# Attention and low-rank mixer on one core: loads in one queue, the first batch reordered, two up blocks begun early, the q gain moved behind the last V, the last tile in three

## The chip, the cores and the metric

The kernel runs on 1 core of one Trainium2 chip. The metric is the device time of one execution in microseconds (us). An execution is also profiled; its time lies beside its span (from the first to the last recorded instruction). The engines are TensorE (PE, matmuls; PEld is its weight load), VectorE (DVE), ScalarE (ACT), GpSimd (POOL) and SyncE (SP, which here only issues DMAs). Each engine works through its own instructions in the order in which the program gives them.

## The reference

```python
# q, k, v: (8, 12, 448, 64); U: (448, 32); V: (32, 448); w_ch1: (768, 3072); w_ch2: (3072, 768)
q_n, k_n = rmsnorm(q, g_q), rmsnorm(k, g_k)            # x / sqrt(mean(x * x) + 1e-6) * g
attn = softmax(q_n @ k_n.T / sqrt(64))                 # by head
x = (attn @ v).transpose(0, 2, 1, 3).reshape(8, 448, 768)
u = x + (x.transpose(0, 2, 1) @ U @ V).transpose(0, 2, 1)
out = u + relu(u @ w_ch1) @ w_ch2                      # float32
```

## The kernel before

**Attention.** The 12 heads of a batch form three groups of four, 24 groups in all; two heads that are worked on together are a pair (`pr`), six pairs in a batch. Per group: `load` brings q, k and v in float32; `squares`, `sums` (L133) and `roots` (L139, L140) give the scale of each row; `scale` or `scale_dma` multiply q and k by it into bfloat16 (`qn`, `kp`); then q and k are transposed into `qT` and `kz`. Groups 0 to 5 are transposed by PE (`turn`) and copied by `take_q`, with the product g_q g_k folded in, and `take_k`. From group 6 on the DMA transposes them (`turn_dma`), and `take_dma` (L341) multiplies `qT` by g_q g_k in place on VectorE. `Sc(b, pr, r)` computes a row block of scores, transposed, two matmuls of 448 columns (L365), and its exponential E on ACT (L366); a pair has four of them, the fourth of half size. `V(b, pr, half)` multiplies E by v with a column of ones (L378, L382), and VectorE takes the reciprocal of the sums (L385) and writes x (L386).

**Mixer and MLP.** For batch 0, `mix_t0` and `mix` compute u transposed (`uT`) on PE, six blocks of 128 of the 768 columns, with copies on ACT or VectorE; for later batches `mix_t` (pu, cast to tb at L401), `mix_tr` (pw, copied to tT at L408) and `mix_rows` (pm, added at L456) compute u, and the DMA transposes it. `up(b, ht)` is one of 24 blocks of the hidden layer: six matmuls over the blocks of `uT` (L466), relu on ACT (L468). `down` computes 128 rows of the output by 384 columns in 24 matmuls (L479), cut into four parts that other work may stand between; VectorE adds u (L487), and two DMAs of 64 rows each on SP's queue write the result (L495), after both halves.

**Order.** The order of the instructions is written out. The first batch's attention is a hand-made list, `extra`, keyed by (pair, row block). After it two lists exist: `att`, the attention of the batches to come, and `mlp`, the mixer and MLP. Each entry has a cost in us, which only serves the planner at the end: it emits the next `att` entry if the costs emitted so far are not ahead of `due`, otherwise the next `mlp` entry. An entry of cost 0 thus follows its predecessor only when the next entry is due: it comes out right in front of that. In the middle of `att`:

```python
        if a == 1 and more and by_dma:
            add_att(0.0, take_dma, gi + 1)
        add_att(0.19, Sc, b, pr, 3)
        if a == 0 and not by_dma:
            add_att(0.0, scale_all, gi + 1)
        if pr != 0:
            add_att(0.55, V, *pairs[i - 1], 1)
```

**Start.** q of group 0 is loaded on SP's queue, k on ACT's, and g_q and g_k behind it on ACT's, then the table of the activation functions. PE runs 115 matmuls on an identity matrix (`keep_busy`, L208) ahead of its first work. VectorE clears the empty parts of `kz` and `vl`, POOL those of Vm (L276), Uz (L290) and tb (L297) while the first data come in.

Of the kernel before, what the change touches and what calls it, by code (L numbers as in the profile page):

```python
# [9 lines left out]
FP32 = mybir.dt.float32  # L10
# [3 lines left out]
ALU = AluOpType  # L14
# [10 lines left out]
def kernel(  # L25
# [13 lines left out]
    nc = tc.nc  # L39
# [14 lines left out]
    D1 = D + 1  # L54
    KD = dm // P
    KH = dh // P
    NPAIR = H // 2
    HALF = dm // 2
    scal = 1.0 / (D ** 0.5)
# [126 lines left out]
    for gi in range(3):  # L186
        stage_tiles(gi)
    load_qk(0, 0)
    load_qk(0, 1, nc.scalar)
    for i, g in enumerate((g_q, g_k)):  # L190
        nc.scalar.dma_start(grow[:, i, :], g.rearrange("(o d) -> o d", o=1))
    for i in range(2):
        load_qk(1, i)
    load_qk(2, 0)
# [16 lines left out]

    eps = consts.tile([P, 1], FP32)
    nc.vector.memset(eps, 1e-6)
    for va, vl in zip(va_bufs, vl_bufs):
# [4 lines left out]
    for t in kz_bufs:  # L219
        for a in range(2):  # L220
            nc.vector.memset(t[D:P, a, :S], 0.0)
            nc.vector.memset(t[0:D, a, S:], 0.0)

    gg = consts.tile([P, 2], FP32)
    bias = gg[:, 1:2]
# [47 lines left out]
    for m in range(NQ):  # L273
        nc.sync.dma_start(Vf[m * rank:(m + 1) * rank, :], moe_V)

    nc.gpsimd.memset(Vm, 0.0)  # L276

    def prep_v(lo, hi):
        for m in range(lo, hi):
# [10 lines left out]
    nc.gpsimd.memset(Uz, 0.0)  # L290
# [5 lines left out]
    for t in tb_bufs:  # L296
        nc.gpsimd.memset(t, 0.0)  # L297


    qk, es, xs = {}, {}, {}  # L300
# [132 lines left out]

    u_rest = consts.tile([P, dm], BF16)

    def urows(b, col, half):
        h = slice(half * HALF, (half + 1) * HALF)
        return u_rest[:, h] if col == SM else xs[b][:, (col - (0 if b % 2 else R)) // P, h]

    def mix_rows(b, w, half):  # L440

        odd = b % 2
# [19 lines left out]
    def up(b, ht):  # L462
# [4 lines left out]
                             start=(dt == 0), stop=(dt == KD - 1))  # L467
        nc.scalar.activation(hT[:, ht, off:off + S], ph, AF.Relu)  # L468

    down_ps, down_sb = {}, {}  # L470

    def down(b, col, half, part, nparts):
        key = (b, col, half)
        if part == 0:
            down_ps[key] = ps.tile([P, HALF], FP32, name="po", tag="ps")
        po = down_ps[key]
        n = KH // nparts
        for ht in range(part * n, (part + 1) * n):
            nc.tensor.matmul(po, hT[:, ht, col:col + P], w2b[:, ht, half * HALF:(half + 1) * HALF],  # L479
                             start=(ht == 0), stop=(ht == KH - 1))  # L480
        if part < nparts - 1:
            return
        h = slice(half * HALF, (half + 1) * HALF)
        if half == 0 or b == 0:
            down_sb[(b, col)] = outp.tile([P, dm], FP32, name="ob", tag="ob")
        ob = down_sb[(b, col)]
        nc.vector.tensor_tensor(ob[:, h], po, urows(b, col, half), ALU.add)  # L487
        if half == 1 or b == 0:
            h = h if b == 0 else slice(0, dm)

            def rows(b, j):
                return out[b].rearrange("(p j) d -> j p d", j=NT)[j]
            for i in range(2):
                o = rows(b, i * NJ + col // P) if col != SM else rows(b - i, 2 * NJ)
                nc.sync.dma_start(o[:, h], ob[i * R:(i + 1) * R, h])  # L495


    pairs = [(b, pr) for b in range(B) for pr in range(NPAIR)]
# [18 lines left out]
    def scales(gi):  # L517
        return [(0, roots, (gi,)), (0, scale, (gi, 0, pool)), (0, scale, (gi, 1, pool))]

    def turns(gi):  # L520
        return [(0.4, turn, (gi, 0)), (0, take_q, (gi, 0)), (0, take_q, (gi, 1)), (0.4, turn, (gi, 1)), (0, take_k, (gi, 0))]
# [4 lines left out]
        (0, 2): [(0, keep_busy, (8,))],  # L526
        (0, 3): [(0, keep_busy, (8,))],
        (1, 1): [V2(0, 0)],
        (1, 2): [(0, sums, (2, 0))] + turns(1),
        (1, 3): [V2(0, 1), (0, sums, (2, 1)), (0, take_k, (1, 1)), (0, values, (1,)), (0, load, (4,)),  # L530
                 (0, weights, (1,))],
        (2, 1): scales(2) + [(0, weights, (1,)), V2(1, 0)],
        (2, 3): [V2(1, 1)],
        (3, 1): [V2(2, 0)],
        (3, 2): turns(2),
        (3, 3): [V2(2, 1), (0, take_k, (2, 1)), (0, values, (2,)), (0, load, (5,)), (0, prep_v, (0, 1)), (0, prep_u, ()),
                 (0, weights, (1,)), (0, squares, (3, 0, pool)), (0, squares, (3, 1, pool)), (0, weights, (1,))],
        (4, 1): [V2(3, 0)],
        (4, 3): [V2(3, 1), (0, sums, (3, 0))],
        (5, 0): [(0.9, mix_t0, (0, 512))],  # L540
        (5, 1): [V2(4, 0), (0.39, mix, (0, 0))],
        (5, 2): [(0.39, mix, (0, 1)), (0.39, mix, (0, 2))],
        (5, 3): [V2(4, 1), (0.39, mix, (0, 3)), (0, prep_v, (1, NQ)), (0, weights, (2,))],
    }
    for i in range(NPAIR):
        for r in range(4):
            add_att(0.38, Sc, *pairs[i], r)
            att.extend(extra.get((i, r), []))
    att.extend([V2(5, 0), V2(5, 1), (0.45, mix_t0, (512, dm, True)), (0, sums, (3, 1)), (0, roots, (3,)),
                (0.39, mix, (0, 4, True)), (0.39, mix, (0, 5))])  # L550
    first_done = len(att)

    att.extend([(0, scale, (3, 0, pool)), (0, scale, (3, 1, nc.vector)), (0, values, (3,)), (1.0, lambda: None, ()), (0.4, turn, (3, 0)), (0.4, turn, (3, 1)),
                (0, take_q, (3, 0)), (0, take_q, (3, 1)), (0, take_k, (3, 0)), (0, take_k, (3, 1))])

    for i, (b, pr) in enumerate(pairs):
        if b == 0:
            continue
        gi, a = divmod(i, 2)
        more = gi + 1 < len(groups)  # L560
        by_dma = gi + 1 >= DMA_FROM
        soon = gi + 2 < len(groups)

        if pr == 0 and b > 1:
            add_att(0.55, V, *pairs[i - 1], 0)
            add_att(0.55, V, *pairs[i - 1], 1)
        add_att(0.38, Sc, b, pr, 0)
        if i == 2 * DMA_FROM - 2:
            add_att(0.0, load, DMA_FROM + 1)
        if a == 0 and not by_dma:  # L570
            add_att(0.0, squares, gi + 1, 0, nc.gpsimd)
            add_att(0.0, squares, gi + 1, 1, nc.gpsimd)
            if gi + 2 >= DMA_FROM:
                add_att(0.0, load, gi + 2)
        add_att(0.38, Sc, b, pr, 1)
        if pr != 0:
            add_att(0.55, V, *pairs[i - 1], 0)
        if a == 1 and more and not by_dma:
# [12 lines left out]
        if a == 1 and more and not by_dma:  # L591
            add_att(0.39, T, gi + 1, 1)
        if a == 1 and more and by_dma:
            add_att(0.0, take_dma, gi + 1)
        add_att(0.19, Sc, b, pr, 3)
        if a == 0 and not by_dma:
            add_att(0.0, scale_all, gi + 1)
        if pr != 0:
            add_att(0.55, V, *pairs[i - 1], 1)
        if a == 1 and soon and gi + 2 >= DMA_FROM:  # L600
            add_att(0.0, sums, gi + 2, 0)
            add_att(0.0, sums, gi + 2, 1)
            add_att(0.0, scale_all, gi + 2)
# [10 lines left out]
    PRE = (16, 20)  # L614
    mlp = []
    for b in range(B):
        for ht in range(KH):
            mlp.append((1.14, up, (b, ht), b))
            if b < ROWS_FROM and ht % 2 == 0 and ht < 4 * NW:
                mlp.append((0.17, mix_rows, (b, ht // 4, ht // 2 % 2), b))  # L620
        cols = (64, 192, 320) if b % 2 == 0 else (384, 0, 128, 256)
        n = len(cols) * 8
        nb = b + 1
        pre = {}
        if ROWS_FROM <= nb < B:
# [5 lines left out]
        tiles = [(col, half) for col in cols for half in range(2)]  # L631
        if b == 0:
            tiles.sort(key=lambda t: t[1])
        for c, (col, half) in enumerate(tiles):
            for part in range(4):
                mlp.extend(pre.get(c * 4 + part, []))
                mlp.append((0.98, down, (b, col, half, part, 4), b))

    for i in range(2):
        squares(0, i)  # L640
# [9 lines left out]
    nc.vector.tensor_copy(gg, pg)  # L650
    squares(1, 0)
    squares(1, 1)
    values(0)
    squares(2, 0, nc.gpsimd,
            uT.rearrange("p k c -> p (k c)")[:, :4 * NT * D].bitcast(FP32).rearrange("p (j d) -> p j d", d=D))
# [86 lines left out]
```

## Time and profile before

| what | value |
|---|---|
| runs | 607.54, 604.35, 608.5 us; median 607.54 |
| profiled execution | 602.04 us, span 600.3 us |
| granted TensorE clock | 1.0 |
| PE / DVE / ACT / POOL busy | 586.2 / 206.6 / 312.5 / 158.5 us |
| matmuls: down (L479), up (L466), scores (L365), V (L382) | 241.6, 237.1, 93.7, 57.2 us |
| first scores on PE | 12.15 us |
| last matmul ends | 595.53 us |

The page gives busy time by engine, then the span in slices, the queues, the chain of work that ended last, and groups of instructions by source line. A timeline line gives start and duration in us, engine, line, operation, output<-input and shape; in brackets stands how long the engine had been idle and what released it. A line of the windows gives the window, its length, busy time of PE, PEld, DVE, ACT and POOL with the number of instructions, the granted clock, the DMA engines' share and GB/s.

### The profile page before, as it was taken

To read this page: it belongs to the slowest core of one execution; us is meant where nothing else is said; L and a number is where in the kernel's file an instruction comes from. 1 tells how busy PE (TensorE), PEld (TensorE's weight loads), DVE (VectorE), ACT (ScalarE), POOL (GpSimd) and SP (SyncE) were. 2 spreads that over 40 slices of the span, in tenths; PEclk is the share of its full clock that TensorE was granted. 3 is DMA by queue.
4 is the path that set the end of the run, shared out by engine and by line. 5 is a ranking of instruction groups with operands and counts; after the bars stand their busy time and mean duration, and the time that the engine had idled before them with its cause. 6 is when DMAs were issued, how large, how long until landed. Compare 5 with 4: busy or idle time off the path is not lost.

```text
span 600.3 us, 11625 instructions
## 1 busy us (share of the span) xinstructions
PE 586.2 (98%) x4807; PEld 357.9 (60%) x4807; DVE 206.6 (34%) x474; ACT 312.5 (52%) x479; POOL 158.5 (26%) x271
## 2 busy tenths in 40 slices
PE   8889999999999999999999999999999999999996
PEld 8555656655666556655566655665566655655563
DVE  6686535511343322531235321541234310320011
ACT  6857873477453776356744477346763344004300
POOL 7997633123213303303303312302312000000000
PEclk9999999999999999999999999999999999999999
DMA  9999996784295454675256746277305310230022
GB/s 257 221 243 246 242 199 160 149 204 96 53 206 107 132 124 113 112 179 123 48 134 99 189 116 139 58 174 169 50 2 89 84 27 0 54 72 2 0 54 52
DMA packets 118360, 71.70 MB, mean 119 GB/s; under 512 B 80420, under 2 KB 115108, under 8 KB 118308
## 3 DMA queue, kind: packets, MB, share of 16 engines
q1 hardware_dynamic: 108304, 61.04, 45.0%
q0 software_dynamic: 9728, 9.47, 9.5%
q8 instruction: 37, 0.61, 0.4%
q10 hardware_dynamic: 276, 0.46, 0.2%
q14 instruction: 15, 0.12, 0.1%
HBM read 52.20 MB, written 11.01 MB: 105 GB/s over the span
## 4 chain that ended last, share of the span: by engine, by line
PE 92%; DVE 3%; ACT 2%; DMA 1%; POOL 1%; issue 0%; POOLq 0%; DVEq 0%; ACTq 0%
PE po L479 36%; PE ph L466 35%; PE sc L365 9%; PE pv L382 5%; PE pm L451 2%; PE pv L378 1%; PE busy L208 1%; ACT E L366 1%; DMA qT<-qn 1%; DVE ssq L133 1%; PE pu L399 1%; PE pt L311 1%; DVE x L386 0%; DVE kz L326 0%; POOL sq L130 0%
## 5 line engine op out<-in xcount | busy, mean ns | idle before, releaser
L479 PE MATMUL po<-w2b,hT 128*128 128x384 bf16 x1344 | 241.6, 326 | 1.0 <-DVE x L386 1.0
L466 PE MATMUL ph<-uT,w1b 128*128 128x448 bf16 x1152 | 237.1, 352 | 0.0
L366 ACT ACTIVATE E<-sc,gg 128x896 bf16<-128x896 f32 x192 | 171.9, 911 | 75.3 <-PE sc L365 75.1
L479 PEld LDWEIGHTS <-hT 128*128 128x128 bf16 x1344 | 126.9, 98 | 79.2 <-DVE x L386 1.1
L466 PEld LDWEIGHTS <-w1b 128*128 128x128 bf16 x1152 | 109.7, 98 | 96.1
L468 ACT ACTIVATE hT<-ph 128x448 bf16<-128x448 f32 x192 | 104.0, 545 | 116.7 <-PE ph L466 114.6
L162 POOL TENSOR_TENSOR qn<-qf,rs 128x384 bf16<-128x384 f32 x36 | 29.9, 830 | 279.1 <-ACT rs L140 225.4
L365 PE MATMUL sc<-qT,kz 128*128 128x448 bf16 x336 | 93.7, 352 | 5.2 <-ACT E L366 3.5
L385 DVE RECIPROCAL r<-pv 128x4 f32<-128x4 f32 x96 | 17.4, 181 | 212.2 <-PE pv L382 211.7
L382 PE MATMUL pv<-va,E 128*128 128x65 bf16 x1152 | 57.2, 194 | 0.0
L487 DVE TENSOR_TENSOR ob<-po,x 128x384 f32<-128x384 f32 x48 | 26.8, 558 | 84.6 <-PE po L479 83.4
L382 PEld LDWEIGHTS <-E 128*128 128x128 bf16 x1152 | 50.5, 98 | 7.5
L133 DVE TENSOR_REDUCE ssq<-sq 128x14 f32<-128x896 f32 x47 | 48.8, 1076 | 2.2 <-ACT sq L128 1.7
L365 PEld LDWEIGHTS <-kz 128*128 128x128 bf16 x336 | 31.8, 98 | 29.1 <-issue 4.7
L378 PE MATMUL pv<-vl,E 128*128 128x130 bf16 x192 | 42.1, 219 | 0.0
L386 DVE TENSOR_TENSOR x<-pv,r 128x256 bf16<-128x256 f32 x96 | 40.8, 425 | 3.3
L139 ACT ACTIVATE rs<-ssq,eps 128x28 f32<-128x28 f32 (+1 forms) x25 | 7.9, 318 | 52.4 <-DVE ssq L133 41.1
L456 DVE TENSOR_TENSOR x<-pm,x 128x384 bf16<-128x384 f32 x48 | 26.6, 554 | 17.9 <-PE pm L451 16.8
L162 POOL TENSOR_TENSOR kp<-kf,rs 128x384 bf16<-128x384 f32 x36 | 29.9, 829 | 0.0
L378 PEld LDWEIGHTS <-E 128*128 128x128 bf16 x192 | 18.7, 97 | 8.1 <-issue 1.2
L170 POOL CAST va<-vf 128x768 bf16<-128x768 f32 x24 | 20.7, 863 | 2.0 <-DMA vf<-in_v_dram 2.0
L128 ACT ACTIVATE sq<-qf 128x896 f32<-128x896 f32 x20 | 18.8, 942 | 2.3 <-DMA qf<-in_q_dram 2.3
(84 smaller groups left out, 265.2 us busy)
## 6 DMA issues: line engine op xcount, KB each, us to landing
qf<-in_q_dram SPq DMA_DIRECT2D x24, 448.0 KB, 4.2
kf<-in_k_dram SPq DMA_DIRECT2D x23, 448.0 KB, 5.5
out_dram<-ob SPq DMA_DIRECT2D x50, 192.0 KB, 2.7
vf<-in_v_dram SPq DMA_DIRECT2D x48, 192.0 KB, 5.4
w1b<-in_moe_w_ch_dram POOLq DMA_DIRECT2D x4, 1152.0 KB, 17.1
w2b<-in_moe_w_ch_dram POOLq DMA_DIRECT2D x8, 576.0 KB, 17.5
vf<-in_v_dram SPq DMA_DIRECT2D x48, 32.0 KB, 4.9
out_dram<-ob SPq DMA_DIRECT2D x12, 96.0 KB, 2.5
```

What stands on the lines that cost most here:

```text
L133: nc.vector.tensor_reduce(ssqs[gi][:, i, :], sqs.pop((gi, i)), AX, ALU.add)
L162: nc.gpsimd.tensor_tensor(main.rearrange("p (t i) d -> p i t d", i=2), src[:, c, :2 * NJ].rearrange("p (i t) d -> p i t d", i=2), rs[:, c, ...
L365: nc.tensor.matmul(sc[:, i, :S], kz[:, c:c + P], qT, start=True, stop=True)
L366: nc.scalar.activation(es[(b, pr)][:, 2 * r:2 * r + n, :], sc[:, :n, :S], AF.Exp, scale=scal, bias=bias)
L378: nc.tensor.matmul(pv[:, i].rearrange("p e d -> p (e d)"), E[:, NJ, w:w + P], vl[:, lp, :], start=True, stop=False)
L382: nc.tensor.matmul(pv[:, i, e, :], E[:, e * (NJ + 1) + j, w:w + P], va[:, (lp + 2 * e) * NJ + j, :], start=False, stop=(e == 1 and j == NJ ...
L386: nc.vector.tensor_tensor(xs[b].rearrange("p i (h d) -> p i h d", d=D)[:, 2 * half:2 * half + 2, h0:h0 + 3:2, :], pv[:, :, :, :D], r.rearr ...
L456: nc.vector.tensor_tensor(dst, ph[lo:hi], x[lo:hi], ALU.add)
L466: nc.tensor.matmul(ph, w1b[:, dt, ht * P:(ht + 1) * P], uT[:, dt, off:off + S], start=(dt == 0), stop=(dt == KD - 1))
L468: nc.scalar.activation(hT[:, ht, off:off + S], ph, AF.Relu)
L479: nc.tensor.matmul(po, hT[:, ht, col:col + P], w2b[:, ht, half * HALF:(half + 1) * HALF], start=(ht == 0), stop=(ht == KH - 1))
L487: nc.vector.tensor_tensor(ob[:, h], po, urows(b, col, half), ALU.add)
```

## The change

There are five parts.

1. The first loads: k of group 0 and g_q, g_k are issued on SP's queue. `fill_k` clears `kz`: the first buffer on VectorE ahead of the other fills, the second on POOL; POOL's fills of Uz, Vm and tb become `fill_mixer`, emitted after the squares of group 1.
2. The first batch: group 1's turns go ahead of its `sums(2, 0)`, `scales(2)` comes at (2, 0) instead of (2, 1), `sums(3, 0)` and the mix blocks come one place later, the fourth mix block is copied by ACT, and `roots(3)` follows the last mix block.
3. `up_begin` runs four of the six matmuls of up blocks 0 and 1 of batch 0 before the mixer of the last four heads is done, into two banks of a score buffer; `up_end` runs the other two and the relu, after up block 2.
4. `take_dma` follows the pair's second V instead of standing in front of the fourth `Sc`.
5. The last output tile is computed in pieces of 384, 192 and 192 columns, each written alone, with the second row half issued on ACT's queue.

```diff
-    load_qk(0, 1, nc.scalar)
+    load_qk(0, 1)
     for i, g in enumerate((g_q, g_k)):
-        nc.scalar.dma_start(grow[:, i, :], g.rearrange("(o d) -> o d", o=1))
+        nc.sync.dma_start(grow[:, i, :], g.rearrange("(o d) -> o d", o=1))
...
+    fill_k(kz_bufs[0], nc.vector)
...
-    nc.gpsimd.memset(Vm, 0.0)
+    fill_k(kz_bufs[1], nc.gpsimd)
...
+    def fill_mixer():
+        nc.gpsimd.memset(Uz, 0.0)
+        nc.gpsimd.memset(Vm, 0.0)
+        for t in tb_bufs:
+            nc.gpsimd.memset(t, 0.0)
...
+    def up_begin(b, ht):
+        off = 64 if b % 2 == 0 else 0
+        if not begun:
+            begin = ps_sc.tile([P, 2, 512], FP32, name="sc", tag="sc")
+            begun.update({(b, i): begin[:, i, :S] for i in range(2)})
+        for dt in range(KD_EARLY):
+            nc.tensor.matmul(begun[(b, ht)], w1b[:, dt, ht * P:(ht + 1) * P], uT[:, dt, off:off + S],
+                             start=(dt == 0), stop=False)
...
-        if half == 1 or b == 0:
-            h = h if b == 0 else slice(0, dm)
+        if hi == dm or alone:
+            h = slice(lo if alone else 0, hi)
...
-                nc.sync.dma_start(o[:, h], ob[i * R:(i + 1) * R, h])
+                (nc.scalar if alone and i and b else nc.sync).dma_start(o[:, h], ob[i * R:(i + 1) * R, h])
...
-        (1, 2): [(0, sums, (2, 0))] + turns(1),
+        (1, 2): turns(1) + [(0, sums, (2, 0))],
...
-        (2, 1): scales(2) + [(0, weights, (1,)), V2(1, 0)],
+        (2, 0): scales(2) + [(0, weights, (1,))],
+        (2, 1): [V2(1, 0)],
...
-        (4, 3): [V2(3, 1), (0, sums, (3, 0))],
+        (4, 3): [V2(3, 1)],
         (5, 0): [(0.9, mix_t0, (0, 512))],
-        (5, 1): [V2(4, 0), (0.39, mix, (0, 0))],
-        (5, 2): [(0.39, mix, (0, 1)), (0.39, mix, (0, 2))],
-        (5, 3): [V2(4, 1), (0.39, mix, (0, 3)), (0, prep_v, (1, NQ)), (0, weights, (2,))],
+        (5, 1): [V2(4, 0), (0, sums, (3, 0))],
+        (5, 2): [(0.39, mix, (0, 0)), (0.39, mix, (0, 1))],
+        (5, 3): [V2(4, 1), (0.39, mix, (0, 2)), (0.39, mix, (0, 3, True)), (0, prep_v, (1, NQ)), (0, weights, (2,))],
...
-    att.extend([V2(5, 0), V2(5, 1), (0.45, mix_t0, (512, dm, True)), (0, sums, (3, 1)), (0, roots, (3,)),
-                (0.39, mix, (0, 4, True)), (0.39, mix, (0, 5))])
+    att.extend([V2(5, 0), V2(5, 1), (0.76, up_begin, (0, 0)), (0.45, mix_t0, (512, dm, True)),
+                (0, sums, (3, 1)), (0.76, up_begin, (0, 1)), (0.39, mix, (0, 4, True)), (0.39, mix, (0, 5)), (0, roots, (3,))])
...
-        if a == 1 and more and by_dma:
-            add_att(0.0, take_dma, gi + 1)
         add_att(0.19, Sc, b, pr, 3)
         if a == 0 and not by_dma:
             add_att(0.0, scale_all, gi + 1)
         if pr != 0:
             add_att(0.55, V, *pairs[i - 1], 1)
+        if a == 1 and more and by_dma:
+            add_att(0.0, take_dma, gi + 1)
...
-        for ht in range(KH):
-            mlp.append((1.14, up, (b, ht), b))
+        for ht in (2, 0, 1, *range(3, KH)) if b == 0 else range(KH):
+            mlp.append((0.38, up_end, (b, ht), b) if b == 0 and ht < 2 else (1.14, up, (b, ht), b))
...
+    for lo, hi in ((0, HALF), (HALF, HALF + 192), (HALF + 192, dm)):
+        mlp.append((3.9 * (hi - lo) / HALF, down, (B - 1, cols[-1], lo, hi, 0, 1, True), B - 1))
...
+    fill_mixer()
     values(0)
```

More of the change, by code (lines that the diff above doesn't have):

```diff
@@ L56 @@
     KH = dh // P
+    KD_EARLY = 4
     NPAIR = H // 2
@@ L213, with fill_k @@
     nc.vector.memset(eps, 1e-6)
+    def fill_k(t, eng):
+        for a in range(2):
+            eng.memset(t[D:P, a, :S], 0.0)
+            eng.memset(t[0:D, a, S:], 0.0)
+    fill_k(kz_bufs[0], nc.vector)
     for va, vl in zip(va_bufs, vl_bufs):
@@ L218 @@
             nc.vector.memset(vl[e * R:(e + 1) * R, :, e * D1 + D:(e + 1) * D1], 1.0)
[L219 to L222, printed above, removed]
     gg = consts.tile([P, 2], FP32)
@@ L289 @@
     tz = first[:, 1, :]
-    nc.gpsimd.memset(Uz, 0.0)
     def prep_u():
@@ L295 @@
     tb_bufs = [consts.tile([P, 2 * P], BF16, name=f"tb{i}") for i in range(2)]
-    for t in tb_bufs:
-        nc.gpsimd.memset(t, 0.0)
+    def fill_mixer():
[3 more added lines that the diff above has]
+            nc.gpsimd.memset(t, 0.0)
     qk, es, xs = {}, {}, {}
@@ L434 @@
     u_rest = consts.tile([P, dm], BF16)
-    def urows(b, col, half):
-        h = slice(half * HALF, (half + 1) * HALF)
-        return u_rest[:, h] if col == SM else xs[b][:, (col - (0 if b % 2 else R)) // P, h]
     def mix_rows(b, w, half):
@@ L468, in up, with up_end, down @@
         nc.scalar.activation(hT[:, ht, off:off + S], ph, AF.Relu)
+    begun = {}
+    def up_begin(b, ht):
[6 more added lines that the diff above has]
+                             start=(dt == 0), stop=False)
+    def up_end(b, ht):
+        off = 64 if b % 2 == 0 else 0
+        for dt in range(KD_EARLY, KD):
+            nc.tensor.matmul(begun[(b, ht)], w1b[:, dt, ht * P:(ht + 1) * P], uT[:, dt, off:off + S],
+                             start=False, stop=(dt == KD - 1))
+        nc.scalar.activation(hT[:, ht, off:off + S], begun[(b, ht)], AF.Relu)
     down_ps, down_sb = {}, {}
-    def down(b, col, half, part, nparts):
-        key = (b, col, half)
+    def down(b, col, lo, hi, part, nparts, alone):
+        key = (b, col, lo)
         if part == 0:
             down_ps[key] = ps.tile([P, HALF], FP32, name="po", tag="ps")
-        po = down_ps[key]
+        po = down_ps[key][:, :hi - lo]
         n = KH // nparts
         for ht in range(part * n, (part + 1) * n):
-            nc.tensor.matmul(po, hT[:, ht, col:col + P], w2b[:, ht, half * HALF:(half + 1) * HALF],
-                             start=(ht == 0), stop=(ht == KH - 1))
+            nc.tensor.matmul(po, hT[:, ht, col:col + P], w2b[:, ht, lo:hi], start=(ht == 0), stop=(ht == KH - 1))
         if part < nparts - 1:
             return
-        h = slice(half * HALF, (half + 1) * HALF)
-        if half == 0 or b == 0:
+        if lo == 0 or b == 0:
             down_sb[(b, col)] = outp.tile([P, dm], FP32, name="ob", tag="ob")
         ob = down_sb[(b, col)]
-        nc.vector.tensor_tensor(ob[:, h], po, urows(b, col, half), ALU.add)
-        if half == 1 or b == 0:
-            h = h if b == 0 else slice(0, dm)
+        u = u_rest if col == SM else xs[b][:, (col - (0 if b % 2 else R)) // P]
+        nc.vector.tensor_tensor(ob[:, lo:hi], po, u[:, lo:hi], ALU.add)
+        if hi == dm or alone:
+            h = slice(lo if alone else 0, hi)
             def rows(b, j):
@@ L548 @@
             att.extend(extra.get((i, r), []))
-    att.extend([V2(5, 0), V2(5, 1), (0.45, mix_t0, (512, dm, True)), (0, sums, (3, 1)), (0, roots, (3,)),
-                (0.39, mix, (0, 4, True)), (0.39, mix, (0, 5))])
+    att.extend([V2(5, 0), V2(5, 1), (0.76, up_begin, (0, 0)), (0.45, mix_t0, (512, dm, True)),
+                (0, sums, (3, 1)), (0.76, up_begin, (0, 1)), (0.39, mix, (0, 4, True)), (0.39, mix, (0, 5)), (0, roots, (3,))])
     first_done = len(att)
-    att.extend([(0, scale, (3, 0, pool)), (0, scale, (3, 1, nc.vector)), (0, values, (3,)), (1.0, lambda: None, ()), (0.4, turn, (3, 0)), (0.4, turn, (3, 1)),
-                (0, take_q, (3, 0)), (0, take_q, (3, 1)), (0, take_k, (3, 0)), (0, take_k, (3, 1))])
+    att.extend([(0, scale, (3, 0, pool)), (0, scale, (3, 1, nc.vector)), (0, values, (3,)), (0.7, lambda: None, ()), (0.4, turn, (3, 0)), (0.4, turn, (3, 1)),
+                (0, take_q, (3, 0)), (0, take_q, (3, 1)), (0, take_k, (3, 0)), (0, take_k, (3, 1)), (0.3, lambda: None, ())])
     for i, (b, pr) in enumerate(pairs):
@@ L630 @@
                     pre[n - PRE[nb > 1] + 2 + 2 * w + half] = [(0.17, mix_rows, (nb, w, half), nb)]
-        tiles = [(col, half) for col in cols for half in range(2)]
+        tiles = [(col, half * HALF, (half + 1) * HALF, b == 0) for col in cols for half in range(2)]
         if b == 0:
             tiles.sort(key=lambda t: t[1])
-        for c, (col, half) in enumerate(tiles):
+        for c, tile_ in enumerate(tiles):
+            if b == B - 1 and c >= len(tiles) - 2:
+                continue
             for part in range(4):
                 mlp.extend(pre.get(c * 4 + part, []))
-                mlp.append((0.98, down, (b, col, half, part, 4), b))
+                mlp.append((0.98, down, (b, *tile_[:3], part, 4, tile_[3]), b))
+    for lo, hi in ((0, HALF), (HALF, HALF + 192), (HALF + 192, dm)):
+        mlp.append((3.9 * (hi - lo) / HALF, down, (B - 1, cols[-1], lo, hi, 0, 1, True), B - 1))
     for i in range(2):
```

## The prediction, made before the changed kernel had run

> **What bounds the kernel now.** I read the page first: busy time by engine, and the chain that ended last.
>
> ```profile
> PE 586.2 (98%) x4807; PEld 357.9 (60%) x4807; DVE 206.6 (34%) x474; ACT 312.5 (52%) x479; POOL 158.5 (26%) x271
> PE 92%; DVE 3%; ACT 2%; DMA 1%; POOL 1%; issue 0%; POOLq 0%; DVEq 0%; ACTq 0%
> ```
>
> TensorE (PE) is busy for all but 14.1 of 600.3 us. No edit takes matmul work away, so the change is worth the idle time that it closes minus the idle time that it opens. The windows tell where there is idle time to close (PE's busy time is the first figure after the window's length).
>
> ```profile
> 0.00:15.00 15.00, 13.15 (x167) 12.15 (x167) 10.50 (x35) 9.12 (x14) 10.96 (x22) 1.00 0.95 257
> 15.00:30.00 15.00, 12.12 (x160) 8.22 (x158) 10.44 (x33) 13.28 (x20) 13.52 (x15) 1.00 0.97 221
> 30.00:45.00 15.00, 12.85 (x144) 8.31 (x144) 13.11 (x26) 8.36 (x14) 14.10 (x18) 1.00 1.14 242
> 180.00:585.00 405.00, 405.00 (x3148) 242.30 (x3147) 114.56 (x251) 197.66 (x306) 71.48 (x143) 1.00 0.42 91
> 585.00:600.30 15.30, 10.52 (x65) 6.12 (x63) 1.68 (x3) 0.00 (x0) 0.00 (x0) 0.99 0.20 51
> ```
>
> About 7 us are lost before 45 us, 4.8 at the end, and nothing in the 405 us between 180 and 585: whatever stalls PE there is paid in full. The timeline names the gaps that the change aims at (the bracket holds the idle time before the line and its releaser).
>
> ```profile
> 38.95 0.39 PE L414 MATMUL pu<-x 128*128 128x256 bf16 x2 [0.44 <-DVE x L386]
> 40.33 0.36 PE L424 MATMUL ph<-Vm,x 128*128 128x448 bf16 x1 [0.46 <-ACT x L416]
> 80.01 0.54 PE L365 MATMUL sc<-qT,kz 128*128 128x448 bf16 x2 [0.60 <-ACT E L366]
> 91.74 0.45 DVE L341 TENSOR_SCALAR qT<-qT,gg 128x896 bf16<-128x896 bf16 x1 [5.18 <-DMA qT<-qn]
> 92.80 4.07 PE L479 MATMUL po<-w2b,hT 128*128 128x384 bf16 x24 [0.98 <-DVE x L386]
> ```
>
> **The change, part by part.**
>
> *Start: 0.* k's load goes behind q's on SP instead of on ACT's queue, g_q and g_k follow on SP, ACT's table load (1.28 us) is no longer behind three issues, and VectorE clears only one kz buffer before its sums. q, k and their scales may come about a microsecond sooner. But PE runs 115 warm-up matmuls until 10.13, then pg and the q turn at 10.67 and the k turn at 11.11; q's scale ends at 10.11 and k's at 11.06. The first scores follow PE's own order, so sooner data bring nothing. If this cover were gone, the gain would be at most the 0.6 us between the end of k's scale and the kz copy at 11.72. On POOL the fills of Uz, Vm and tb (0.57 + 1.85 + 0.61 = 3.0 us) move behind q's scale, 10.11 at the latest, so they end between 11.6 and 13.1; the cast of v, at 12.07 now, is used only after some rows of scores. I take 0, with -0.6 to +0.5.
>
> *First batch: 0.* The turns of group 1 ahead of sums(2, 0) release the scores at 20.55 about 0.5 sooner (wait on kz: 0.52). Against it, roots(2) now stands on ACT in front of E of the same rows and waits for sums(2, 1), 2 x 1.08 us on VectorE behind the copies: E comes about 1.1 later, of which 0.5 falls into ACT's idle time. sums(3, 0) leaves the place ahead of the tz copy, which frees the 0.62 wait at 34.74. Sum -0.1, rounded to 0; bounds -0.6 to +0.7.
>
> *Two up blocks begun: -1.1, lost again by 80.* Eight matmuls (4 of 6 in each block; six take 1.14 at L466, so 8 x 0.19 = 1.52 us) go into the idle 0.44 + 0.15 + 0.46 at 38.95 to 40.33. That is all they can fill: 1.05. They remove no work. After it roots(3) stands behind the last mix copy, so q's scale on POOL (1.69 from 41.18 now) ends later while its turn comes sooner; of the gain some is waited out there, but the 0.48 wait for kz at 46.11 goes. I get PE 1.1 further by 46. Then comes a chain whose length PE does not set: from the turn of k at 72.38 through the kz copies, the clearing of kp (0.81), V's pair, two sums (2.07), roots(6) and E, to the scores at 80.01, 7.63 us. PE waits 0.60 there now. With PE further on in the up blocks, one block fewer (1.14) lies inside that chain, so the wait grows by that: 0.60 + 1.14 = 1.74. I keep -0.1 of -1.1 (bounds -1.1 and +0.8, where the wait at the turns of group 3 stays).
>
> *g_q g_k behind the last V: -1.0, then +6.1.* take_dma (L341, one VectorE multiply, 0.44 us, x18) moves from ahead of the fourth row of scores to behind the second V. Today at 86.5 it waits 5.18 us for a DMA, and V's pair of L385 and L386 behind it keeps PE waiting 0.98 at 92.80. In the new order V goes first, so this 0.98 is won, once; at no other L341 does VectorE wait for a DMA.
>
> But the multiply now stands directly in front of the scores that need it, behind whatever VectorE has just been given. Reading the new order of PE and VectorE beside each other, group by group, I counted the matmuls between the source of the VectorE operation ahead of the multiply and the new group's first scores. In the old order there were 3.6 us or more of them. In the new one there are none for groups 7, 10, 13 (a down block's add ahead) and 19 (the tb cast ahead). The place for group 7 is visible already:
>
> ```profile
> 112.14 2.11 PE L479 MATMUL po<-w2b,hT 128*128 128x384 bf16 x12
> 114.09 0.54 PE L365 MATMUL sc<-qT,kz 128*128 128x448 bf16 x2
> ```
>
> ```profile
> 111.16 0.44 DVE L341 TENSOR_SCALAR qT<-qT,gg 128x896 bf16<-128x896 bf16 x1
> 114.29 0.56 DVE L487 TENSOR_TENSOR ob<-po,x 128x384 f32<-128x384 f32 x1 [1.31 <-PE po L479]
> 114.76 2.07 DVE L133 TENSOR_REDUCE ssq<-sq 128x14 f32<-128x896 f32 x2
> ```
>
> The scores start at 114.09, since qT was multiplied 3 us before. In the new order the multiply sits between L487 and L133: it starts at 114.76 as L133 does now, takes 0.44, and some 0.05 later (as the kz copy of 11.72, 0.38 long, frees the scores at 12.15) the scores start: 114.76 + 0.44 + 0.06 - 114.09 = 1.17. Groups 10 and 13 have the same rows (add at 180.48 and 247.00, scores at 180.28 and 246.80): 3 x 1.17 = 3.5. Group 19 has the cast (0.36) in the add's place: 1.0. Groups 17, 20 and 22 have one quarter of a down block (0.98) between: 1.17 - 0.98 = 0.2 each, 0.6. Group 23 has an add and a half u_rest add ahead, and 1.15 of matmuls: 0.5. In group 16 the two sums (2.07) now lie between the tb cast and the tT copy, which pm waits for: 0.4. The other groups have 2 us or more of matmuls there: 0. Sum 3.5 + 1.0 + 0.6 + 0.5 + 0.4 = 6.0, less 0 for cover, since PE idles nowhere in that stretch. Bounds: 2.3 (each of the four bare places gets a quarter of a down block, 0.2) and 7.
>
> *The last tile in 384, 192, 192: -1.2.* After PE's last matmul (595.53) there are now:
>
> ```profile
> 595.56 0.56 DVE L487 TENSOR_TENSOR ob<-po,x 128x384 f32<-128x384 f32 x1 [3.34 <-PE po L479]
> ```
>
> then two SP issues that end at 596.61 and 597.25, and landings at 598.76 and 599.34. The last add shrinks to 192 columns: 0.36, as the cast of 192 columns, -0.2. The second issue goes to ACT's queue, beside the first: -0.6. The pieces shrink from 192 KB; the page has 2.7 us from issue to landing for 192 KB and 2.5 for 96 KB, so -0.2 at least, and -1.0 if the last bytes at 300 GB/s bound the end (393 KB in 1.3 us, 98 KB in 0.3). 24 more matmuls of half width add 0.05. Sum -0.95 to -1.75; I take -1.2. The Trainium skill's DMA: Bandwidth & Descriptors (Rules for kernel authors) says that transfers under 64 KB pay mostly overhead; the new pieces have 48 KB, and by it the byte term would be 0 and the sum -0.75. The 0.2 between the two rows here leans its way, but no 48 KB row stands in this trace.
>
> **Sum:** 0 + 0 - 0.1 - 1.0 + 6.0 - 1.2 = +3.7 us on the profiled execution's 602.04 (span 600.3): 605.7. The runs of before have their median at 607.54, 5.5 above that execution; the same +3.7 there gives 611.2.
>
> **Rivals.**
> *Faster or level: the bare places are covered.* If PE has something else at the four places (the order of the down quarters slips by one as PE's lead changes) each costs 0.2: 0.8 + 0.6 + 0.5 + 0.4 = 2.3, all 0.0, 607.5. If the multiply never delays scores, the sum is -2.3: 605.2; if, besides, the early lead is kept at 80 (-1.1 for -0.1) and the end gives 1.75, -3.9: 603.6. For it: scores of groups that start with two V's have cover. Against it: both engines' orders are fixed in the program, and the rows at 114 leave no room. It decides at group 7's first scores.
> *Slower still: the early stage.* roots(2) and roots(3) are later on ACT, and POOL, 13 to 14 us busy in each 15 us there, gets the fills late. If the kept -0.1 becomes +0.8, the first batch +0.7, the start +0.5 and a split end only -0.75, the sum is +3.7 + 2.5 + 0.45: +6.7, 614.2. For it: ACT and POOL at 13.28 and 13.52 of 15. Against it: PE's gaps of before 45 us belong to several waits, and one delay is often paid by another's slack.
> *The begun blocks fill nothing:* PE then reaches 80 later with a shorter wait there, so the end hardly moves: +3.8, 611.3. It shows only in the early gaps.
>
> **Chances.** Forecast (+1 to +6) 0.55; covered, level or faster 0.17; slower still 0.25; the rest 0.03. A measurement of this kernel tells about 1% (6 us) from no change. Over 1% faster needs more than the whole first rival: 0.08. Over 1% slower is the second rival and the upper edge of the forecast: 0.32. Within 1%: 0.60. The range runs from the first rival's lower end, 604, to 617, above the second rival by the 7 for 6 of the multiply and 2 for what I may not have seen.
>
> **What would show it.** Right: PE idle of 1.1 to 1.2 us ahead of the first scores of groups 7, 10 and 13, released by qT's multiply, and about 1.0 at group 19; no 0.98 at 92.8; a larger wait for E near 80; the span 0.8 to 1.8 us shorter behind the last matmul; 180 to 585 no longer full. Wrong: that stretch still full of PE (then the first rival), or over 3 us more idle before 90 (then the second).

## The result, and the profile after

The changed kernel takes 613.0 us (median of 5 runs, 612.04 to 614.22) beside 606.9 us for the kernel before (604.35 to 608.5): ratio 1.0105, interval 1.0074 to 1.0137. A second set of runs gave 610.9 beside 604.58 us: 1.0108 (1.0081 to 1.0134). The prediction was 611.2 in a range of 604 to 617. Its profiled execution took 612.44 us (span 610.7), 10.4 more than the shown one of before, but that one was among the fastest of before, whose later runs lie between 601.4 and 608.2 us. So the sum of the steps is to be judged by the 6 us of the medians, and its terms by the traces.

The page of the changed kernel: more idle time on PE, less PE in the chain that ended last.

```profile
PE 588.2 (96%) x4830; PEld 359.0 (59%) x4831; DVE 205.2 (34%) x470; ACT 313.3 (51%) x480; POOL 160.0 (26%) x275
PE 89%; DVE 3%; DMA 2%; issue 2%; ACT 1%; POOL 1%; SPq 0%; POOLq 0%; DVEq 0%
```

Its windows (PE's busy time first, the granted clock third from the end): 15 to 30 lost 2.5 us more than before, 45 to 60 lost 1.9 more with the clock at 0.89, and the stretch behind 100, which was full, is no longer full (87.89 of 90 us in the last line).

```profile
15.00:30.00 15.00, 9.67 (x126) 6.45 (x126) 8.06 (x22) 10.79 (x15) 13.66 (x12) 1.00 0.95 229
30.00:45.00 15.00, 13.39 (x163) 8.84 (x160) 12.72 (x30) 9.37 (x15) 11.78 (x18) 1.00 1.14 242
45.00:60.00 15.00, 12.26 (x78) 6.55 (x77) 7.66 (x17) 8.94 (x15) 8.99 (x8) 0.89 1.14 243
180.00:270.00 90.00, 87.89 (x733) 53.69 (x731) 32.59 (x70) 47.70 (x71) 21.96 (x44) 1.00 0.57 126
```

The timeline of PE has the gaps by place (idle time before the line in brackets):

```profile
18.42 0.56 PE L317 MATMUL pt<-ident,qn 128*128 128x128 bf16 x7 [0.88 <-POOL qn L144]
20.07 0.56 PE L317 MATMUL pt<-ident,kp 128*128 128x128 bf16 x7 [1.08 <-POOL kp L144]
25.89 0.35 PE L371 MATMUL sc<-qT,kz 128*128 128x448 bf16 x1 [2.51 <-ACT E L372]
47.38 0.56 PE L317 MATMUL pt<-ident,qn 128*128 128x128 bf16 x7 [2.08 <-POOL qn L144]
85.99 0.54 PE L371 MATMUL sc<-qT,kz 128*128 128x448 bf16 x2 [1.74 <-ACT E L372]
120.14 0.54 PE L371 MATMUL sc<-qT,kz 128*128 128x448 bf16 x2 [1.06 <-issue]
187.55 0.54 PE L371 MATMUL sc<-qT,kz 128*128 128x448 bf16 x2 [1.06 <-issue]
255.29 0.54 PE L371 MATMUL sc<-qT,kz 128*128 128x448 bf16 x2 [1.06 <-issue]
388.80 0.54 PE L371 MATMUL sc<-qT,kz 128*128 128x448 bf16 x2 [0.86 <-issue]
479.07 0.54 PE L371 MATMUL sc<-qT,kz 128*128 128x448 bf16 x2 [0.63 <-issue]
```

The last five are groups 7, 10, 13, 19 and 23. "issue" hides the releaser: VectorE's timeline at the first of them has it.

```profile
119.12 0.56 DVE L507 TENSOR_TENSOR ob<-po,x 128x384 f32<-128x384 f32 x1 [1.31 <-PE po L500]
119.59 0.45 DVE L347 TENSOR_SCALAR qT<-qT,gg 128x896 bf16<-128x896 bf16 x1
119.95 2.07 DVE L134 TENSOR_REDUCE ssq<-sq 128x14 f32<-128x896 f32 x2
```

The multiply (L347 now) starts 0.47 after the add and ends at 120.04; the scores start at 120.14. It is the picture that the prediction drew from before, 0.45 us inserted between L487 and L133. The end: the last matmul ends at 606.91, the span at 610.7, so 3.79 us instead of 4.78.

Since all kernels here run the same exponentials E in the same order on ACT, the start of the n-th E beside the shown profile of before tells where a kernel is ahead (-) or behind (+), in us:

| kernel | first E (12.74) | pair 5, first E (32.49) | batch 1, first E (46.70) | pair 9, last E (74.55) | batch 2, first E (97.89) | last E (486.61) |
|---|---|---|---|---|---|---|
| changed | -0.72 | +2.27 | +6.33 | +5.94 | +4.83 | +11.33 |
| changed, second profile | +0.03 | +1.21 | +4.68 | +4.29 | +3.18 | +9.68 |
| before, second profile | -0.66 | -0.66 | -0.66 | -0.66 | +4.48 | +4.48 |

From the first E of batch 2 to the last E both profiles of the changed kernel lose the same 6.50 us. The rest differs from execution to execution, in both kernels.

### The profile page after: what moved, and what is told of

Same layout as the page of the kernel before. It is cut to its first block, busy times and chain, and to the rows that moved or that the text cites. A ratio compares the mean times of both kernels' runs of the same rounds, so it can differ in the third digit from the quotient of the medians.

```text
span 610.7 us, 11683 instructions
## 1 busy us (share of the span) xinstructions
PE 588.2 (96%) x4830; PEld 359.0 (59%) x4831; DVE 205.2 (34%) x470; ACT 313.3 (51%) x480; POOL 160.0 (26%) x275
## 4 chain that ended last, share of the span: by engine, by line
PE 89%; DVE 3%; DMA 2%; issue 2%; ACT 1%; POOL 1%; SPq 0%; POOLq 0%; DVEq 0%
PE po L500 35%; PE ph L468 35%; PE sc L371 9%; PE pv L388 5%; DMA vf<-in_v_dram 2%; PE pm L453 2%; PE pv L384 2%; DVE ssq L134 1%; ACT E L372 1%; PE pu L405 1%; PE pt L317 1%; POOL qn L144 0%; SPq L93 0%; DVE x L295 0%; DVE kz L332 0%
## 5 line engine op out<-in xcount | busy, mean ns | idle before, releaser
L500 PE MATMUL po<-w2b,hT 128*128 128x384 bf16 (+1 forms) x1368 | 241.6, 323 | 0.0
L500 PEld LDWEIGHTS <-hT 128*128 128x128 bf16 x1368 | 128.7, 98 | 77.2
L507 DVE TENSOR_TENSOR ob<-po,x 128x384 f32<-128x384 f32 (+1 forms) x49 | 26.9, 549 | 92.3 <-PE po L500 92.1
```

Source lines behind the costliest of these rows:

```text
L500: nc.tensor.matmul(po, hT[:, ht, col:col + P], w2b[:, ht, lo:hi], start=(ht == 0), stop=(ht == KH - 1))
L507: nc.vector.tensor_tensor(ob[:, lo:hi], po, u[:, lo:hi], ALU.add)
```

## The experiments

Each result gives the median of the kernel and, beside it, the median of the kernel before in the same set of runs, then the ratio with its 95% interval. The ratio is not exactly the quotient of the two medians.

**The multiply's place, undone** (`take_dma_back`):

```diff
+        if a == 1 and more and by_dma:
+            add_att(0.0, take_dma, gi + 1)
         add_att(0.19, Sc, b, pr, 3)
...
-        if a == 1 and more and by_dma:
-            add_att(0.0, take_dma, gi + 1)
```

> The changed kernel with the multiply of qT by g_q g_k alone put back in front of the fourth row of scores. Theory A (the multiply stands bare in front of the scores that need it): PE's idle time of 1.06 three times, 0.86 and 0.63 us ahead of the first scores of groups 7, 10, 13, 19 and 23 goes, with the few tenths at 16, 17, 20 and 22, some 6 us; the wait of V behind a DMA near 100 us may come back, up to 1.0. So 5 to 6 us faster than the changed kernel, ratio to before about 1.001. Rival B (PE's time is set elsewhere, the stalls only move): under 1 us faster.

604.51 beside 603.33 us, ratio 1.0019 (1.0000 to 1.0038): 0.9% below the changed kernel's 1.0105 and 1.0108, 5.3 us. PE idles nowhere between 100 and 585 us; near 95 it waits 0.18 for V. Theory A holds.

**The multiply's place alone, in the kernel before** (`take_dma_alone`; the reverse edit):

> The kernel before with the one edit that the multiply of qT stands behind the second V. The planner's places differ from the changed kernel's: here six groups (7, 10, 13, 20, 22, 23) have no matmul between a down block's add and the new group's first scores, and two (16, 19) none behind the tb cast. Theory A (the bare multiply is paid in full): 6 x 1.1 + 2 x 0.9 + 0.2 = 8.6 us of PE idle time between 100 and 585 us, where the kernel before has none, so more than the 6 of the changed kernel; against it the wait of V behind the DMA near 93 us (0.98 in one profile of before, 3.25 with 7 us at half clock in the other) is gone. Span about 607 to 609, ratio to before 1.005 to 1.012. Rival B (the multiply's place costs little, and the changed kernel's loss has another source): no idle time there, and a ratio of 0.99 to 1.00, since the wait near 93 goes.

611.82 beside 604.1 us, 1.0132 (1.0105 to 1.016), the slowest kernel of all; span 608.8. The gaps came at the eight places counted, six of 1.06 and two of 0.86 us:

```profile
114.35 0.54 PE L365 MATMUL sc<-qT,kz 128*128 128x448 bf16 x2 [1.06 <-issue]
315.93 0.54 PE L365 MATMUL sc<-qT,kz 128*128 128x448 bf16 x2 [0.86 <-issue]
406.58 0.54 PE L365 MATMUL sc<-qT,kz 128*128 128x448 bf16 x2 [1.06 <-issue]
```

Its first E of batch 2 is 0.95 us ahead of before, so the 0.98 was won; its last matmul is 8.61 behind (604.13 beside 595.52), which makes 9.56 lost against 8.6 expected. The eight brackets sum to 8.08, and a gap of 0.08 at group 17 is too short to be listed. The other 1.4 us are no idle time, but fit the refilling of PE behind each of the nine gaps: one matmul of the scores alone takes 0.35 us in the timeline and two in a row 0.54, so each break costs an estimated 0.16 us more than its bracket. The same edit costs 9.6 here and 6.5 in the changed kernel because the planner there puts a quarter of a down block in front of the scores in other groups.

**The roots of group 3** (`roots3_back`):

```diff
-                (0, sums, (3, 1)), (0.76, up_begin, (0, 1)), (0.39, mix, (0, 4, True)), (0.39, mix, (0, 5)), (0, roots, (3,))])
+                (0, sums, (3, 1)), (0, roots, (3,)), (0.76, up_begin, (0, 1)), (0.39, mix, (0, 4, True)), (0.39, mix, (0, 5))])
```

> The changed kernel with roots(3) put back in front of the last two mix blocks, the only edit. Theory A (behind the mix copies the roots of group 3 come at 44.07 us and leave POOL idle for 2.94 us; PE then waits 2.08 us for the q scale, and the granted clock falls to 0.5 for about 4 us): the roots come about 1 us sooner, the wait of 2.08 shrinks to about 1, and the clock stays at 1.00; 2 to 4 us faster than the changed kernel. If the clock falls all the same, 1 us faster. Rival B (POOL waits for a load of group 3, not for the roots): nothing changes, within 0.5 us.

608.71 beside 603.33 us, 1.0075 (1.0045 to 1.0106), some 1.9 us below the changed kernel; the intervals overlap, so the trace has to show it. The wait of 2.08 for the q scale is down to 0.22:

```profile
45.18 0.56 PE L317 MATMUL pt<-ident,qn 128*128 128x128 bf16 x7 [0.22 <-POOL qn L144]
```

Between the first E of pair 5 and that of batch 1 this kernel loses nothing against before (2.67 and 2.60 us behind), where the changed kernel loses 4.06 and 3.47 us in its two profiles. The clock fell all the same, but elsewhere: behind the wait of 2.51 near 25. Theory A for the wait; for the clock, neither.

**The scales of group 2** (`scales2_back`):

```diff
-        (2, 0): scales(2) + [(0, weights, (1,))],
-        (2, 1): [V2(1, 0)],
+        (2, 1): scales(2) + [(0, weights, (1,)), V2(1, 0)],
```

> The changed kernel with the scales of group 2 put back one row of scores later, behind the second E of pair 2; nothing else. Theory A (the roots stand on ACT in front of an E that PE needs, and wait there for sums on VectorE): the wait of 2.51 us for E near 25 us shrinks to under 0.5, and 1.5 to 2.5 us are gained, 3 or more if the half clock behind one of the two long gaps goes too. Rival B (PE is held by E's order of arrival anyway, the wait moves to the next rows or to the turns of group 2, whose scale comes later): under 0.7 us gained.

609.32 beside 604.1 us, 1.0093 (1.0066 to 1.0121), about 0.8 below the changed kernel, which is less than the intervals can tell apart. The 2.51 became 0.36, but two rows on PE waits 1.30 for VectorE:

```profile
23.16 0.35 PE L371 MATMUL sc<-qT,kz 128*128 128x448 bf16 x1 [0.36 <-ACT E L372]
25.31 1.06 PE L371 MATMUL sc<-qT,kz 128*128 128x448 bf16 x4 [1.30 <-DVE r L391]
```

So between the two, and nearer to Rival B: half of the wait moved to the next rows. The other half is the roots' place.

**The queues of the first loads** (`queue_back`):

```diff
-    load_qk(0, 1)
+    load_qk(0, 1, nc.scalar)
     for i, g in enumerate((g_q, g_k)):
-        nc.sync.dma_start(grow[:, i, :], g.rearrange("(o d) -> o d", o=1))
+        nc.scalar.dma_start(grow[:, i, :], g.rearrange("(o d) -> o d", o=1))
```

> The changed kernel with k of group 0, g_q and g_k loaded on ACT's queue again, the only edit. Theory A (five issues in a row on SP leave the DMA engines short of work at 4 to 6 us, so v of group 0 lands at 13.50 instead of 12.01, the v cast holds up POOL's queue, and q's and k's scales of group 1 come 1.3 us late): v lands about 1.4 us sooner, the waits of PE for POOL at the turns of group 1 (0.88 and 1.08 us) shrink to under 0.4 each, the wait for E near 25.9 (2.51 us) by about as much as the turns come sooner, and the kernel is 1 to 3 us faster than the changed one. Rival B (the new order of the first batch makes these waits by itself): v lands sooner, but PE waits as long near 18, 20 and 26 us; under 0.5 us faster.

610.55 beside 603.33 us, 1.0116 (1.0084 to 1.0147): nothing gained. v of group 0 landed at 11.34 us, against 13.50 and 11.92 in the two profiles of the changed kernel. The profile lacks the waits for POOL near 18 and 20, but so does the second profile of the changed kernel, so these belong to the execution, not to the queue. The wait near 25 stays at 2.54. Theory A falls. The Trainium skill's DMA: Bandwidth & Descriptors (Rules for kernel authors) says that other queues give no bandwidth and only save issue time; here even the issue time had no effect that could be measured.

**The kernel before, again** (`before_again`):

> The kernel before, unchanged, to have a second profile of it: its shown profile took 602.04 us, its runs have a median of 606.9. Theory A: executions differ in the first 100 us, where landings of loads set the order of waits, so a profile near 606 has 3 to 5 us more PE idle time before 100 us and the same 405.00 us of 405.00 from there on. Rival B: the difference is spread over the span, a few tenths in each 90 us.

603.78 beside 603.33 us. Its profile took 606.75 us, and the 5.1 us by which it falls behind the shown one between pair 9 and batch 2 are at one place. Timelines of PE and VectorE, then windows:

```profile
94.42 5.94 PE L479 MATMUL po<-w2b,hT 128*128 128x384 bf16 x18 [3.25 <-DVE x L386]
```

```profile
93.36 0.45 DVE L341 TENSOR_SCALAR qT<-qT,gg 128x896 bf16<-128x896 bf16 x1 [7.46 <-DMA qT<-qn]
```

```profile
90.00:92.00 2.00, 1.16 (x19) 0.82 (x16) 0.00 (x0) 0.00 (x0) 0.00 (x0) 1.00 1.36 144
92.00:94.00 2.00, 0.00 (x0) 0.00 (x0) 0.61 (x3) 0.00 (x0) 0.00 (x0) 0.86 1.31 212
94.00:100.00 6.00, 5.58 (x18) 2.72 (x19) 3.84 (x8) 0.55 (x2) 2.85 (x5) 0.50 0.88 236
```

The wait of V behind the multiply and its DMA is 3.25 us here, and PE comes out of it at half clock for 6 us. Theory A holds for the place: PE still idles nowhere between 100 and 585 us. Of the 5.1 us only 2.2 are more idle time before 100 us, where 3 to 5 were expected; the rest is the half clock. So the 0.98 that the prediction took for the worth of the multiply's move was one draw of a quantity that varies.

**The begun up blocks alone** (`up_begin_alone`; `up_begin`, `up_end` and the lists that call them, in the kernel before):

> The kernel before with the two begun up blocks alone (roots(3) stays where it was). Theory A (given back at the chain to the scores near 80 us): the gaps of 0.44, 0.15 and 0.46 us near 39 to 40 close, PE is about 1 us further near 46, and the wait for E near 80 grows from 0.60 to about 1.7, so that PE is within 0.3 us of before at the first scores of batch 2. Ratio 0.997 to 1.002. Rival B (the lead is kept): wait near 80 still 0.6 and 1 us gained there.

605.76 beside 604.58 us, 1.0004 (0.998 to 1.0029). The gaps near 39 and 40 are gone, and the lead is given back:

```profile
79.39 0.54 PE L366 MATMUL sc<-qT,kz 128*128 128x448 bf16 x2 [1.74 <-ACT E L367]
94.60 5.62 PE L498 MATMUL po<-w2b,hT 128*128 128x384 bf16 x17 [3.40 <-DVE x L387]
```

0.60 + 1.14 = 1.74, to the hundredth what the prediction worked out. The first E of batch 2 is 4.74 us behind the shown profile of before, but within 0.3 us of the second one (4.48), which has the long wait near 94 too. The change's third part is worth nothing that can be measured.

**The last tile alone** (`last3_alone`; the fifth part of the change, in the kernel before):

> The kernel before with the last tile alone in 384, 192 and 192 columns and the second row half on ACT's queue. Theory A (0.2 of a shorter add, 0.6 of an issue beside the other): the stretch from PE's last matmul to the end of the span shrinks from 4.78 to about 3.8 us, ratio 0.998 to 0.999. Rival B (48 KB pieces pay a fixed cost that eats it): 4.4 or more.

602.82 beside 604.1 us, 0.9981 (0.9956 to 1.0005). The last matmul ends at 595.31, the span at 599.1: 3.8 instead of 4.78. Theory A.

**The clearing of kp** (`kp_pool`; with the last tile in three):

```diff
-                nc.vector.memset(kp, 0.0)
+                nc.gpsimd.memset(kp, 0.0)
```

> The kernel before with the last tile in 384, 192, 192 and the clearing of kp for the transposes by DMA on POOL instead of VectorE. Theory A (the clearing, 0.81 us on VectorE, is a link of the chain from the turn of k to the scores near 80 us): the wait of 0.60 near 80 is gone, 0.6 us more than the last tile alone gives. Rival B (the chain runs over ACT and PE, not over VectorE): the wait stays at 0.6.

601.98 beside 604.58 us, 0.9968 (0.9945 to 0.9991). The wait near 80 is gone, so the clearing was a link of that chain. But behind it stands the DMA, for 2.70 us (94.14). Against the last tile alone, 0.9981, the intervals overlap, so the times do not show that the clearing's move is worth anything.

**Three edits in the kernel before** (`best2`: begun up blocks, last tile, kp on POOL):

> The kernel before with three edits: the two begun up blocks, the last tile in 384, 192, 192, and the clearing of kp on POOL. Theory A (the chain to the scores near 80 decides what is kept of the early gain): the wait near 80 is 0.60 + 1.1 - 0.8 = 0.9 us, so 0.8 us of PE's lead is kept until 90; the wait behind the DMA near 92 takes no more than that; 1.0 at the end. Ratio to before 0.995 to 0.998. Rival B (the landings of the transposes near 92 us pin PE there): only the 1.0 of the end is kept, ratio 0.998 to 0.999.

604.0 beside 604.58 us, 0.9995 (0.9974 to 1.0017). The wait near 80 is 0.70 where 0.9 was expected, but

```profile
95.98 4.34 PE L499 MATMUL po<-w2b,hT 128*128 128x384 bf16 x13 [5.90 <-DVE x L387]
```

So Rival B, and more than it said: the transposes of group 6 do not land at a fixed time; in these five profiles they land later when they are issued earlier. The trace's issue of the first, the landing of the second q transpose, and the landing of the last w2b load:

| kernel | issued | q landed | last w2b landed |
|---|---|---|---|
| best2 | 79.55 | 94.89 | 95.05 |
| kp_pool | 80.65 | 93.06 | 92.62 |
| before, second profile | 80.69 | 93.33 | 92.80 |
| before, shown profile | 81.34 | 91.72 | 90.71 |
| last3_alone | 81.53 | 91.44 | 90.33 |

In all five the q transpose lands within 1.2 us of the end of the w2b loads, and both come later the sooner the transposes join them (the two that are issued within 0.04 us of each other aside). That they share the DMA engines fits (share 1.30 or 1.31 in 75 to 90 us); no run took the w2b loads away, so this cause stays argued.

**The changed kernel without its three losses** (`combined`: `roots3_back`, `scales2_back`, and the multiply behind V for group 6 alone):

> The changed kernel with roots(3) back in front of the last two mix blocks, the scales of group 2 back behind the second E, and the multiply of qT behind the second V for group 6 alone, in front of the fourth row of scores for the others. Theory A (what was lost early and between 100 and 585 us has these three sources): PE idles nowhere from 100 to 585; the early gaps of 2.5 and 2.1 us are gone, so that no clock falls to half; span about 598, ratio 0.988 to 0.995. Rival B (the early gaps come back elsewhere, since the chain to the scores near 80 us gives back what PE gains): ratio 0.997 to 1.002.

601.28 beside 604.1 us, 0.9961 (0.9942 to 0.9979): between the two expectations, and faster than before and the changed kernel; with `kp_pool` one of the two versions whose interval lies below 1. PE idles nowhere from 100 to 585 us and the clock is 1.00 throughout, as Theory A has it; but waits of 1.33 us near 24 and 1.74 near 79 stay, as Rival B has it. Its runs lie closer together (600.15 to 603.29) than those of before beside it (601.87 to 606.51): with the multiply of group 6 behind V, the DMA, through what stands behind the multiply on VectorE, holds PE up for 1.06 + 0.40 us in its profile, with no half clock. Its first E of batch 1 is 0.22 ahead, that of batch 2 level (+0.07): the gain is the end and the missing long wait.

**The changed kernel, again** (`after_again`):

> The changed kernel, unchanged, beside the others on one chip. Theory A (its losses have a fixed place in the order of instructions): 1.06 us three times, 0.86 and 0.63 between 100 and 585 us, 2.5 near 25 and 1.74 near 85 as in its first profile, and one fall of the clock to half behind one of the gaps of 2 us or more; ratio to before 1.008 to 1.014. Rival B (landings decide): these gaps differ by half a microsecond or more between the two profiles.

610.9 beside 604.58 us. 1.06 three times, 0.86, 0.63, 2.53 and 1.74 stand at the same places, so they are of the order; the waits for POOL at 18 and 20 are absent, so they are not.

## Why the prediction was right, point by point

*The multiply, +6.0.* Right in place, mechanism and size: predicted 1.17 three times, 1.0, 0.5 and small ones; idle time 1.06, 0.86, 0.63; 6.5 us from batch 2 to the end; 5.3 by the ratios when undone. The predicted figures are delays of the scores; with the estimated 0.16 of refilling the idle times become delays of 1.22, 1.02 and 0.79.

*Its gain, -1.0.* Right in kind, mis-sized. The term came from one profile; the wait that it removes was 0.18 to 5.90 us in the profiles of kernels with the old order, with half clock behind those of 3.25 and more. In the median execution of before this term is probably larger than 1.0: its medians in the later sets, 603.3 to 604.6 us, lie 1.3 to 2.5 above the execution from which the term was read. Which part of that arises at this wait is shown for the second profile alone.

*The end, -1.2.* Measured -0.99 in the changed kernel and -1.0 alone: inside the bounds of 0.95 to 1.75 and near the smaller, in which the byte term is the 0.2 between the profile's rows of 192 and 96 KB. From the end of the last issue to the end of the span it is 3.01 us before and 2.83 after, so the smaller pieces did save 0.2, and the sum of -0.75, with a byte term of 0, did not come. The rate of 300 GB/s behind the larger bound was assumed: from 598 to 599 us the shown profile of before moves 237 GB/s.

*The begun blocks, -0.1.* Right when taken alone: 1.74 us near 80 in every kernel with them, but `best2`, where the chain was shortened.

*The first batch, 0.* The step that failed first. The prediction let half of E's delay fall into ACT's idle time; PE waited 2.51 for that E. By pair 5 the changed kernel has lost 1.2 us in one profile and 3.0 in the other, which also has the two waits for POOL (0.88 and 1.08). `scales2_back` takes half of the 1.2 away (0.6 are left).

*The turns of group 3.* The step that failed most: "some is waited out there" was counted as nothing. With roots(3) behind the last mix copy POOL stood idle for 2.94 us, and PE waited 2.08 for the q scale:

```profile
44.07 0.32 ACT L140 ACTIVATE rs<-ssq,eps 128x28 f32<-128x28 f32 x1
44.79 2.53 POOL L144 TENSOR_TENSOR qn<-qf,rs 128x896 bf16<-128x896 f32 x1 [2.94 <-issue]
50.40 2.16 PE L468 MATMUL ph<-uT,w1b 128*128 128x448 bf16 x6
```

The third line is six matmuls that take 1.30 elsewhere: half clock. The later roots are not all of it. In the five profiles with the roots behind the last mix block POOL's multiply takes 2.53 or 2.54 us, in the nine others 1.68 or 1.69, which is what the prediction reckoned with; VectorE's multiply of k, which runs beside it, takes 1.09 in the five and 1.83 to 1.95 in the nine. Why POOL is slower there stays open.

This is the second rival, the early stage, which was given 0.25. Its sign, over 3 us more idle time before 90, came in one profile (5.4 more) and was just missed in the other (2.9). Its own sum is off: +0.9, +0.7 and +0.5 make 2.1 and not 2.5, so it stood for 613.8 and not 614.2. That the runs gave 613.0 does not confirm its prices: the early loss was two to three times its 2.1.

*The sum.* +3.7 was forecast and +6.1 measured, just above the +1 to +6 that the prediction held likeliest; the ratios of 1.0105 and 1.0108 lie just beyond 1% slower, to which it gave 0.32. That the time of 611.2 came within 2 us is partly luck, since two misses went against each other: the early loss up to pair 9 was 4 to 7 us (6.66 and 4.26 in the two profiles) instead of none, and the gain at the DMA's wait, in the median execution, probably larger too. That the early loss partly runs into that wait is seen in `take_dma_back`: 3.42 behind at pair 9, it waits 0.18 there where before waits 0.98, and is 2.67 behind at batch 2.

## What to carry to other kernels

An instruction that costs nothing in a planner's list comes out directly in front of the next costed one; if that one needs its result, count the work between what stands ahead of it on its engine and the consumer, place by place. A gain read from one profile at a wait for a DMA is one draw: profile the kernel twice before it becomes a term. And where PE's progress is pinned further on by landings, time won ahead of it comes back as waiting.

## What the runs showed of the hardware

The clock falls behind gaps of well under 3 us, and not always. Behind 2.08 us of idle and a few matmuls PE ran at 0.50 from 49 to 52 us in the changed kernel; `scales2_back` had the same gap of 2.09 and kept 1.00; `roots3_back` and `take_dma_back` fell behind the 2.51 near 25, where the changed kernel, with the same 2.51, kept 1.00; `kp_pool` kept 1.00 behind 2.70.

What differs is where the gap lies. In the traces' records of the granted clock every fall that begins before the last matmul ends lasts 3.41 or 6.83 us, and it starts a whole number of steps of 3.413 us after the record's start. In the changed kernel the record starts at 4.34 us and the fall comes 13 steps later. Its windows, cut along these steps:

```profile
21.41:24.82 3.41, 1.70 (x20) 0.97 (x19) 3.28 (x8) 1.51 (x4) 2.38 (x5) 1.00 1.08 288
24.82:28.24 3.42, 2.29 (x33) 1.58 (x33) 1.51 (x6) 3.32 (x5) 3.15 (x2) 1.00 1.12 243
45.30:48.72 3.42, 1.11 (x10) 0.70 (x11) 1.14 (x3) 0.77 (x2) 3.32 (x4) 1.00 1.14 236
48.72:52.13 3.41, 3.18 (x14) 1.73 (x14) 2.47 (x9) 0.72 (x2) 3.32 (x2) 0.50 1.15 223
```

The gap of 2.51 is split over two steps, with 1.71 and 1.13 us of idle time, and nothing falls. The gap of 2.08 lies in one step, with 2.31 us of idle time in all, and the next step runs at 0.50. In the fourteen profiles every full step at clock 1.00 with 2.03 us or more of idle time was followed by half clock, and none with 1.78 or less; where between the two the limit lies is not shown. The waits of 3.25, 3.40 and 5.90 us all fell, for two steps. The Trainium skill's TensorE: Matmul & The Clock Gate (Part 1) has a free-running activity window of about 3.4 us, and these steps agree. Its advice (Why this matters for your kernels) that gaps above some 3 us are to be avoided is too lenient here, where 2.08 us were enough.

The same 115 warm-up matmuls took 7.99 to 9.27 us in these profiles. They stand 105 ns apart until 4.2 to 7.0 us and 56 ns apart from then on, and the first scores came between 11.44 and 12.55 us, later where this change came later.
